# Attention units of four heads instead of two, a softmax in eight portions and a written order on all engines, in a fused attention and MoE kernel

## The chip, the cores and the metric

The kernel runs on one core of a Trainium2 chip. The metric is the device time of one execution in microseconds (us). The engines are named as in the profile: PE (TensorE: matrix products, PEld its weight loads), DVE (VectorE), ACT (ScalarE), POOL (GpSimd) and SP (SyncE, which here only issues transfers).

## The reference, cut to what matters

Eight batches of eight heads, 512 local and 32 global tokens, head width 64; a local token sees the keys within 32 places of it and the 32 global ones, a global token sees all 544. The result, 4608 tokens by 512, goes through a gated feed-forward layer.

```python
k_all = np.concatenate([k_g, k_l], axis=2); v_all = np.concatenate([v_g, v_l], axis=2)
out_g = sm(scale * q_g @ k_all.T) @ v_all                    # global tokens
s_ll = np.where(np.abs(pos[:, None] - pos[None, :]) <= 32, scale * q_l @ k_l.T, -1e9)
out_l = sm(np.concatenate([scale * q_l @ k_g.T, s_ll], -1)) @ v_all   # local tokens
# x: both as rows of 512 (8 heads x 64)
xn = x / sqrt(mean(x * x) + 1e-6) * rms_g
g = xn @ w_gate
return (g * sigmoid(g) * (xn @ w_val)) @ w_out               # 512 -> 1536 -> 512
```

## The kernel before

**Chunks.** The tokens go through the feed-forward part (MoE) in nine chunks: chunks 0 to 7 are the local tokens of one batch each (512), chunk 8 the 256 global ones. The attention of chunks 0 and 1 runs at the head of the program, together with the conversion of the weights, in an order written by hand; that head ends about 171 us in, and the diff leaves its work alone. From then on PE works on the MoE of chunk c, and the attention of chunk c+1 is put between its products. The change concerns the attention of chunks 2 to 7, so six chunks, and the global units that lie between.

**MoE of a chunk.** 72 half-steps of six dense products (128 rows by 512 columns, fp16, each operand split into a high and a low part): for each of twelve feature tiles f two half-steps of the gate product (bank `p0`) and two of the value product (`p1`), then 24 half-steps of the output product. Behind a tile's gate product ACT takes the tanh (`moe_gate`), DVE makes the gate from it ("gate"); behind its value product DVE multiplies (`moe_h`, "inner"), ACT casts the high part, POOL subtracts for the low part. `p0` has one PSUM bank, so the next tile's gate product waits until "gate" has read it, and the same holds for `p1` and "inner".

**Slots.** After each half-step `slot()` may issue steps of the attention from the list `todo`. A step is ready when its unit's first slot has come (`UNIT`) and when the steps it names are a given number of slots back; at most one step that uses PE goes into a slot. So in a chunk the places before are: local units start at slots 0, 20, 30 and 40 and the global one at 10; for the first unit loads L at slot 0, scores S at 4, values A at 11; for the global unit scores GS at 14, transposes GT at 19, values GA at 23, the turn GX at 26.

**A local unit before** (`local_quarters`) has two heads and a quarter of the sequence on each 32 partitions. S: 64 products of 32 query rows by 128 keys into two PSUM banks. Softmax, issued with S: per 128 columns DVE adds the mask and takes the minimum of the negated scores, ACT takes the exponential and its sum, adds a small number to the sums, DVE inverts them, POOL multiplies 128x512 by them, DVE transposes in blocks of 32. A: per block of keys and quarter a product for each head into four banks, 56 products of one to four query tiles (32 columns each). A product in fp32 appears in the trace as two matmul records in A, as one in S. Then four DVE copies of 128x128 and the squares on ACT, summed by POOL. `attn_bank` hands out four PSUM banks; scores, values, GS and GA all take them, and each waits until a bank has been read empty.

**Order.** PE and SP run in the order in which the program is written. DVE, ACT and POOL are ordered by a scheduler from chunk 1 on, with the MoE's instructions ahead (`HIGH`).

Of the kernel before, what the change touches and what calls it, by code (L numbers as in the profile page):

```python
# [9 lines left out]
F32 = mybir.dt.float32  # L10
# [55 lines left out]
def attention_moe_kernel(  # L66
# [37 lines left out]
    with tc.high_priority(100000):  # L104
        mask = con.tile([P, 4 * P], F32, tag="mask", name="mask")
# [315 lines left out]
    def local_unit(c, hp):  # L421
# [12 lines left out]
        def load():  # L434
# [4 lines left out]
            else:  # L439
                q = pool.tile([P, SL], F32, tag="q", name=f"q{u}")  # L440
                k = pool.tile([P, KU], F32, tag="k", name=f"k{u}")
# [69 lines left out]
        def copies(h):  # L511
            st["pt", h] = pool.tile([P, 512], F32, tag="pt", bufs=2, name=f"pt{u}{h}")
            nc.scalar.copy(st["pt", h], st["t", h])

        def values():
            ps = st["a"] = bank(f"a{u}", "pg" if hp % 2 == 0 else "pv")
            for g in range(4):
                for h in range(2):
                    for a in range(4):
# [4 lines left out]
                            st["pt", h][:, i * QT : (i + 1) * QT],  # L524
# [39 lines left out]
    def local_quarters(c, b, hp, xt):  # L564
        u = b * (H // 2) + hp
        w = u - EARLY * (H // 2)
        st = {}

        def load():
            if w == 0:  # L570
                late["mask"] = con.tile([P, 4 * P], F32, tag="mask", name="maskb")
                nc.sync.dma_start(late["mask"], maskb)
                nc.sync.dma_start(same, eyes)
            q = pool.tile([P, SL], F32, tag="q", name=f"q{u}")
            nc.sync.dma_start(q, qkb[w, :, :SL])
            k = pool.tile([P, 1024], F32, tag="v", bufs=4, name=f"k{u}")[:, : 4 * KB]
            nc.sync.dma_start(k, qkb[w, :, SL:])
            v = pool.tile([P, 1024], F32, tag="v", bufs=4, name=f"v{u}")[:, : 4 * KB]
            nc.sync.dma_start(v, vb[w])
            st.update(q=q, k=k, v=v)  # L580

        def softmax(h, ps):
            sm = st["sm"]
            e = pool.tile([P, 4, P], F32, tag="e", bufs=4, name=f"e{u}{h}")
            for g in range(4):
                cols = slice(g * P, (g + 1) * P)
                nc.vector.tensor_tensor_reduce(  # L587
                    out=e[:, g, :],
                    in0=ps[:, cols],
                    in1=late["mask"][:, cols],  # L590
# [4 lines left out]
                    accum_out=sm[:, 0, 4 * h + g : 4 * h + g + 1],  # L595
                )
            for g in range(4):
                j = 4 * h + g
# [4 lines left out]
                    bias=sm[:, 0, j : j + 1],  # L603
                    scale=-1.0,
                    accum_out=sm[:, 1, j : j + 1],
                )
            r = sm[:, 2, 4 * h : 4 * h + 4]
# [652 lines left out]
```

## Time and profile before

| | |
|---|---|
| time, median of 3 executions | 976.73 us (976.18 to 977.36) |
| the profiled execution | 977.08 us, its span 975.1 us |
| mean granted TensorE clock | 0.989 of full speed |
| PE | 940.9 us busy, 96% of the span |
| DVE, ACT, POOL | 457.9, 403.1 and 198.2 us busy |

The profile shows one execution; the 2 us between its time and its span lie before the first and after the last instruction. An engine's busy time is the union of its instructions. PE's matmuls are pipelined: a record is longer than the distance to the next one, so the distance of two starts is what a product costs.

### The profile page before, as it was taken

To read this page: it belongs to the slowest core of one execution; us is meant where nothing else is said; L and a number is where in the kernel's file an instruction comes from. 1 tells how busy PE (TensorE), PEld (TensorE's weight loads), DVE (VectorE), ACT (ScalarE), POOL (GpSimd) and SP (SyncE) were. 2 spreads that over 40 slices of the span, in tenths; PEclk is the share of its full clock that TensorE was granted. 3 is DMA by queue.
4 is the path that set the end of the run, shared out by engine and by line. 5 is a ranking of instruction groups with operands and counts; after the bars stand their busy time and mean duration, and the time that the engine had idled before them with its cause. 6 is when DMAs were issued, how large, how long until landed. Compare 5 with 4: busy or idle time off the path is not lost.

```text
span 975.1 us, 24168 instructions
## 1 busy us (share of the span) xinstructions
PE 940.9 (96%) x10308; PEld 489.4 (50%) x10308; DVE 457.9 (47%) x1417; ACT 403.1 (41%) x1070; POOL 198.2 (20%) x183
## 2 busy tenths in 40 slices
PE   6588999999999999999999999999999999999998
PEld 4444455455445554455445454455445544444584
DVE  6999973434344443434343534434433534332231
ACT  7999982344133431444133531445134421332131
POOL 0000000223112331223131331233121421112020
PEclk9699999999999999999999999999999999999999
DMA  9972420800053101700052101610071102400100
GB/s 358 405 260 87 157 89 33 267 31 21 23 155 109 51 2 41 245 31 21 23 179 87 50 13 62 214 50 2 24 224 56 35 12 99 126 1 1 44 1 22
DMA packets 31258, 90.55 MB, mean 93 GB/s; under 512 B 3632, under 2 KB 3888, under 8 KB 31152
## 3 DMA queue, kind: packets, MB, share of 16 engines
q1 hardware_dynamic: 30720, 88.68, 27.0%
q8 instruction: 81, 1.33, 0.6%
q10 hardware_dynamic: 432, 0.33, 0.1%
q14 instruction: 25, 0.20, 0.1%
HBM read 80.09 MB, written 8.91 MB: 91 GB/s over the span
## 4 chain that ended last, share of the span: by engine, by line
PE 86%; DVE 6%; DMA 5%; ACT 2%; issue 0%; SPq 0%; ACTq 0%; DVEq 0%
PE p L896 48%; PE po L945 24%; PE a L658 4%; PE po L1010 3%; PE s L626 3%; DMA k<-in_qk_dram 2%; DMA v<-in_vw_dram 1%; DMA wr<-in_w_in_dram 1%; PE ga L763 1%; PE gt L749 1%; PE gs L710 1%; DVE wf L366 1%; ACT wr L265 1%; DMA gkq<-in_gkq_dram 1%; DVE t L979 1%; DMA k<-in_qkb_dram 1%
## 5 line engine op out<-in xcount | busy, mean ns | idle before, releaser
L896 PE MATMUL p<-xh,wf 128*128 128x512 f16 (+1 forms) x1728 | 505.5, 368 | 6.9 <-DVE t L979 6.3
L896 PEld LDWEIGHTS <-wf 128*128 128x128 f16 x2592 | 248.8, 98 | 275.9 <-issue 19.9
L896 PE MATMUL p<-xl,wf 128*128 128x512 f16 (+1 forms) x864 | 317.9, 368 | 0.2 <-DVE xl L821 0.2
L945 PE MATMUL po<-wo,h 128*128 128x512 f16 x1080 | 236.4, 379 | 0.0
L151 POOL TENSOR_TENSOR h<-t,h 128x512 f16<-128x512 f32 (+1 forms) x96 | 105.2, 1095 | 463.4 <-ACT h L917 460.8
L945 PEld LDWEIGHTS <-h 128*128 128x128 f16 x1080 | 105.1, 98 | 124.5
L907 DVE SCALAR_TENSOR_TENSOR t<-t,p 128x512 f32<-128x512 f32 (+1 forms) x96 | 62.4, 650 | 162.8 <-ACT t L906 162.8
L917 ACT CAST h<-t 128x512 f16<-128x512 f32 (+1 forms) x96 | 56.6, 589 | 147.2 <-DVE t L914 147.2
L906 ACT ACTIVATE t<-p,half_inv 128x512 f32<-128x512 f32 (+1 forms) x96 | 62.9, 655 | 124.7 <-PE p L896 109.7
L914 DVE SCALAR_TENSOR_TENSOR t<-t,c_h,p 128x512 f32<-128x512 f32 (+1 forms) x96 | 68.5, 714 | 72.4 <-PE p L896 72.3
L599 ACT ACTIVATE e<-e,sm 128x128 f32<-128x128 f32 x192 | 74.3, 389 | 44.1 <-DVE sm L587 44.1
L610 POOL TENSOR_TENSOR e<-e,sm 128x512 f32<-128x512 f32 x48 | 49.1, 1039 | 130.9 <-DVE sm L609 106.0
L587 DVE CUSTOM_DVE_ANT_0 e<-s,maskb 128x128 f32<-128x128 f32 x192 | 42.5, 286 | 38.5 <-PE s L626 38.5
L957 DVE TENSOR_SCALAR o<-po,kk 128x512 f32<-128x512 f32 x15 | 11.3, 751 | 103.6 <-PE po L945 103.6
L886 ACT CAST xh<-x 128x512 f16<-128x512 f32 x24 | 14.0, 615 | 82.7 <-DVE x L883 82.7
L613 DVE STREAM_TRANSPOSE et<-e 128x512 f32<-128x512 f32 x48 | 34.1, 710 | 25.1 <-POOL e L610 25.1
L658 PEld LDWEIGHTS a<-et,v 32*64 32x64 f32 x2688 | 35.5, 130 | 10.2 <-issue 10.2
L151 POOL TENSOR_TENSOR xl<-x,xh 128x512 f16<-128x512 f32 x12 | 18.6, 1549 | 98.3 <-ACT xh L886 98.3
L669 ACT ACTIVATE sq<-x 128x512 f32<-128x512 f32 x24 | 15.1, 630 | 56.6 <-DVE x L667 56.6
L658 PE MATMUL a<-et,v 32*64 32x64 f32 (+3 forms) x2688 | 38.2, 242 | 0.0
L599 ACT ACTIVATION_READ_ACCUMULATOR e<-e,sm 128x1 f32 x192 | 36.1, 188 | 0.0
L667 DVE COPY x<-a 128x128 f32<-128x128 f32 x96 | 21.2, 283 | 24.6 <-PE a L658 24.6
(320 smaller groups left out, 752.8 us busy)
## 6 DMA issues: line engine op xcount, KB each, us to landing
wr<-in_w_in_dram SPq DMA_DIRECT2D x24, 512.0 KB, 9.7
k<-in_qkb_dram SPq DMA_DIRECT2D x24, 448.0 KB, 6.8
v<-in_vb_dram SPq DMA_DIRECT2D x24, 448.0 KB, 5.0
gkq<-in_gkq_dram SPq DMA_DIRECT2D x16, 576.0 KB, 6.6
out_dram<-o SPq DMA_DIRECT2D x34, 256.0 KB, 2.0
v<-in_vw_dram SPq DMA_DIRECT2D x16, 512.0 KB, 9.9
gv<-in_gv_dram SPq DMA_DIRECT2D x16, 448.0 KB, 10.2
wr<-in_w_out_dram SPq DMA_DIRECT2D x12, 512.0 KB, 4.5
```

What stands on the lines that cost most here:

```text
L151: nc.gpsimd.tensor_tensor(dst, a, b, ALU.subtract)
L587: nc.vector.tensor_tensor_reduce(out=e[:, g, :], in0=ps[:, cols], in1=late["mask"][:, cols], scale=-0.125, scalar=3.0e38, op0=ALU.add, op1 ...
L599: nc.scalar.activation(e[:, g, :], e[:, g, :], AF.Exp, bias=sm[:, 0, j : j + 1], scale=-1.0, accum_out=sm[:, 1, j : j + 1],)
L610: nc.gpsimd.tensor_tensor(e, e, r.unsqueeze(2).to_broadcast([P, 4, P]), ALU.mult)
L613: nc.vector.transpose(st["et", h], e.rearrange("p g k -> p (g k)"))
L658: nc.tensor.matmul(o, st["v"][a * QT : (a + 1) * QT, m * P + h * D : m * P + (h + 1) * D], x, start=(m == blocks[0]), stop=(m == blocks[-1 ...
L896: nc.tensor.matmul(ps[:, :n], wf[f][:, a, o : o + P], ch[z][k][:, :n], start=(k == 0 and i == 0), stop=(k == NK - 1 and i == 2),)
L906: nc.scalar.activation(t[:, :n], pg[:, :n], AF.Tanh, scale=half_inv[:, f : f + 1])
L907: nc.vector.scalar_tensor_tensor(t[:, :n], t[:, :n], 1.0, pg[:, :n], ALU.add, ALU.mult)
L914: nc.vector.scalar_tensor_tensor(t[:, :n], t[:, :n], c_h[:, f : f + 1], pv[:, :n], ALU.mult, ALU.mult)
L917: nc.scalar.copy(h[:, 0, :n], t[:, :n])
L945: nc.tensor.matmul(ps[0], ch["h", f][:, a, j * P : (j + 1) * P], wo[f][:, z, :], start=(f == 0 and q == 0), stop=(f == NF - 1 and q == 2),)
```

## The change

From chunk 2 on a local unit (`local_halves`) has four heads, as two pairs (z), with half a sequence on each 32 partitions; a chunk has two such units instead of four. The keys of a score product come from both pairs' tiles, so S (128 products, four banks) needs the queries and keys of both; the values are a load of their own (V). A pass over values has 11 blocks of keys (88 products for four heads; 112 before): the first block, the global keys, serves eight query tiles (256 columns), the others three, two or one. They run in two pieces, A (5 blocks) and B (6). The copies are of 128x256, two for each pair: X for the first, Y for the second. The softmax is cut into eight portions, M0, N0 to M3, N3 (two times 128 columns each), with the division D and the transposes T of a bank as steps of their own. The same steps of a chunk now stand at: loads 0 and 2, S 6, M0 7, N0 8, M1 9, D0 and N1 10, M2 11, T0, D1 and N2 12, M3 13, T1, D2 and N3 14, T2 and D3 16, T3 18, A 19, B 21, X 22, GS 23, Y 24, then the globals' softmax GM 24 and GN 26, GT 29, GA 33, GX 36, and the second unit's S 37, A 50, B 52, X 53, Y 55.

All five engines run in the written order. In it the half-step's products come first, then the slot's steps, then the gate, inner or store that belongs to the half-step (`rest`). The norm's last part issues its four scalings, four casts and four subtractions together, in three groups. The mask has six instead of four blocks of 128 columns (393 KB instead of 262, loaded once).

```diff
-    HIGH = 10
+    SPLIT, BGAP = 5, 2
-    UNIT = {0: 0, 2: 20, 3: 16, 4: 12, 5: 10, 6: 9, 7: 8}
+    UNIT = {2: (0, 20), 3: (2, 19, 33)}
...
-    def local_quarters(c, b, hp, xt):
+    def local_halves(c, b, hp, xt):
...
+            for z in range(2):
+                q = pool.tile([P, SL], F32, tag="q", name=f"q{u}{z}")
+                nc.sync.dma_start(q, qkb[2 * w + z, :, :SL])
+                k = pool.tile([P, 1024], F32, tag="v", bufs=4, name=f"k{u}{z}")[:, : 4 * KB]
+                nc.sync.dma_start(k, qkb[2 * w + z, :, SL:])
...
+        def divide(x, bk):
...
             nc.vector.reciprocal(r, r)
             nc.gpsimd.tensor_tensor(e, e, r.unsqueeze(2).to_broadcast([P, 4, P]), ALU.mult)
...
+            ps = [[attn_bank(f"s{u}{x}{bk}") for bk in range(2)] for x in range(2)]
...
+            for t in range(8):
+                bk, g = divmod(t, 4)
+                for z in range(2):
+                    for half in range(2):
...
+                            nc.tensor.matmul(
+                                ps[x][bk][p : p + QT, g * P : (g + 1) * P],
+                                st["q"][z][r, i * QT : (i + 1) * QT],
+                                st["k"][z][r, k0 : k0 + P],
...
+        blocks = (10, 2, 3, 4, 5, 6, 7, 1, 8, 0, 9)
+
+        def values(ms):
...
+            for m in ms:
+                for p in range(4):
+                    r = slice(p * QT, (p + 1) * QT)
+                    for x in range(2):
+                        lo, n, e = queries(st["et"][x][r], m)
...
-            for a in range(4):
-                nc.vector.tensor_copy(xt[hp][:, a * P : (a + 1) * P], ps[a][:, :P])
...
+        def take(z):
...
+            for half in range(2):
+                nc.vector.tensor_copy(
+                    x[:, half * 256 : (half + 1) * 256], st["a"][2 * z + half][:, :256]
+                )
...
+            ("L", load, 0, [("^S", 0)]),
+            ("V", load_v, 0, [("^B", 0)]),
+            ("S", scores, 1, [("L", LG[0]), ("^Y", 1)]),
+        ]
+        for j, (x, bk) in enumerate(((0, 0), (1, 0), (0, 1), (1, 1))):
+            steps += [
+                (f"M{j}", lambda x=x, bk=bk: softmax(x, bk, (0, 1)), 0, [("S", 2 * j + 1)]),
+                (f"N{j}", lambda x=x, bk=bk: softmax(x, bk, (2, 3)), 0, [(f"M{j}", 1)]),
+                (f"D{j}", lambda x=x, bk=bk: divide(x, bk), 0, [(f"N{j}", 2)]),
+                (f"T{j}", lambda x=x, bk=bk: turn(x, bk), 0, [(f"D{j}", 2)]),
+            ]
+        return steps + [
+            ("A", lambda: values(blocks[:SPLIT]), 1, [("T3", 1), ("V", 4)]),
+            ("B", lambda: values(blocks[SPLIT:]), 1, [("A", BGAP)]),
+            ("X", lambda: take(0), 0, [("B", 1)]),
+            ("Y", lambda: take(1), 0, [("X", 2)]),
         ]
...
-            ("GT", transp, 1, [("GS", GG[1])]),
+            ("GM", lambda: softmax(0), 0, [("GS", 1)]),
+            ("GN", lambda: softmax(1), 0, [("GM", 2)]),
+            ("GT", transp, 1, [("GN", GG[1] - 2)]),
             ("GA", values, 1, [("GT", GG[2])]),
-            ("GX", turn, 1, [("GA", GG[3])]),
+            ("GD", divide, 0, [("GA", 1)]),
+            ("GX", turn, 1, [("GD", GG[3] - 1)]),
...
-            if i == 1:
-                if w == 0:
-                    ps["t"] = moe_gate(f, n, ps[0])
-                else:
-                    moe_h(ch, f, n, ps["t"], ps[1], on)
...
+        return [
+            (lambda: half(0, 0), None),
+            (lambda: half(0, 1), gate),
+            (lambda: half(1, 0), None),
+            (lambda: half(1, 1), inner),
+        ]
...
-    ctx.enter_context(tc.manual_schedule(engines={eng.PE, eng.SP}))
-    with tc.manual_schedule(engines={eng.DVE, eng.Activation}):
-        for name in ORDER.split():
-            job.pop(name)()
+    every = {eng.PE, eng.SP, eng.DVE, eng.Activation, eng.Pool}
+    ctx.enter_context(tc.manual_schedule(engines=every))
+    for name in ORDER.split():
+        job.pop(name)()
...
-        for k, w in enumerate(work):
-            with tc.high_priority(HIGH):
-                w()
+        for k, (products, rest) in enumerate(work):
+            products()
...
+            if rest:
+                rest()
```

DVE around the first copies of chunk 2, before; `a80` to `a83` are the four banks of A's result, `t2` and `t3` feature tiles 2 and 3, `gs000` and the like a global unit's four score banks:

```order
L907 SCALAR_TENSOR_TENSOR t2_2337<-t2_2337,p0_2_2324 128x512
L914 SCALAR_TENSOR_TENSOR t2_2337<-t2_2337,c_h_78,p1_2_2340 128x512
L667 COPY x2_0_2367<-a80_2368 128x128
L667 COPY x2_0_2367<-a81_2369 128x128
L667 COPY x2_0_2367<-a82_2370 128x128
L667 COPY x2_0_2367<-a83_2371 128x128
L907 SCALAR_TENSOR_TENSOR t3_2447<-t3_2447,p0_3_2434 128x512
L719 ISA ge0_2458,gsm0_2457<-gs000_2459,zeros_73 128x272
```

The same engine after, from the gate of tile 5 on, with the copies of X (`x2_0`) and Y (`x2_1`):

```order
L970 SCALAR_TENSOR_TENSOR t5_2592<-t5_2592,p0_5_2531 128x512
L704 COPY x2_0_2602<-a40_2473 128x256
L704 COPY x2_0_2602<-a41_2474 128x256
L977 SCALAR_TENSOR_TENSOR t5_2592<-t5_2592,c_h_78,p1_5_2595 128x512
L704 COPY x2_1_2645<-a42_2475 128x256
L704 COPY x2_1_2645<-a43_2476 128x256
L774 ISA ge0_2614,gsm0_2613<-gs000_2615,zeros_73 128x272
L774 ISA gsm0_2613 128x1
L774 ISA ge0_2614,gsm0_2613<-gs001_2616,zeros_73,gsm0_2613 128x272
```

Before, the four copies freed all of A's banks in one go, ahead of the gate of tile 3 and of the first reader of GS. Now X's two copies and Y's two have the inner of tile 5 between them, and GM, the first reader of GS, stands directly behind Y. On PE the eight GS products into `gs000` and `gs010` (which take the banks that X frees) and then the eight into `gs001` and `gs011` (those that Y frees) stand directly behind the last half-step of tile 5, the one that inner reads.

ACT in chunk 2, the first unit's softmax before; L599 are exponentials, L608 the small addition, L906 tanh, L917 casts:

```order
L917 CAST h0_2225<-t0_2209 128x512
L599 ACTIVATE e80_2271,sm8_2236<-e80_2271,sm8_2236 128x128 x4
L599 ACTIVATE e81_2285,sm8_2236<-e81_2285,sm8_2236 128x128
L906 ACTIVATE t1_2305<-p0_1_2229,half_inv_77 128x512
L599 ACTIVATE e81_2285,sm8_2236<-e81_2285,sm8_2236 128x128 x3
L608 ACTIVATE sm8_2236<-sm8_2236 128x4 x2
L917 CAST h0_2225<-t1_2305 128x512
```

ACT after, in the middle of the same softmax (L610, L619, L969 and L980 are the same four operations; `e410`, `e401` and `e411` three of the four banks, `t2` and `t3` tiles 2 and 3):

```order
L610 ACTIVATE e410_2350,sm4_2247<-e410_2350,sm4_2247 128x128 x2
L969 ACTIVATE t2_2355<-p0_2_2332,half_inv_77 128x512
L610 ACTIVATE e410_2350,sm4_2247<-e410_2350,sm4_2247 128x128 x2
L619 ACTIVATE sm4_2247<-sm4_2247 128x4
L610 ACTIVATE e401_2378,sm4_2247<-e401_2378,sm4_2247 128x128 x2
L980 CAST h2_2383<-t2_2355 128x512
L610 ACTIVATE e401_2378,sm4_2247<-e401_2378,sm4_2247 128x128 x2
L619 ACTIVATE sm4_2247<-sm4_2247 128x4
L610 ACTIVATE e411_2408,sm4_2247<-e411_2408,sm4_2247 128x128 x2
L969 ACTIVATE t3_2413<-p0_3_2387,half_inv_77 128x512
L610 ACTIVATE e411_2408,sm4_2247<-e411_2408,sm4_2247 128x128 x2
L619 ACTIVATE sm4_2247<-sm4_2247 128x4
```

Before, eight exponentials stood around one tanh, and the rest of the chain was the MoE's own; now sixteen stand in pairs between the tanh and the casts of tiles 1 to 3, and each engine keeps to this order whichever operand is ready first.

## Rows read from the trace of the kernel before

**Rows 1.** Table by stage: 250 to 550 us, three stretches of 100, summed.

```profile
sum 300.00, PE 299.69 PEld 149.46 DVE 126.17 ACT 101.54 POOL 76.73; mean PE 99.90 PEld 49.82 DVE 42.06 ACT 33.85 POOL 25.58
```

**Rows 2.** Chain of waits, one chunk: start us, us, what, records.

```profile
387.88 6.47 PE p L896 x30
394.36 1.09 PE s L626 x64
...
404.62 1.52 PE a L658 x77
406.14 3.99 PE p L896 x18
...
417.79 1.09 PE gt L749 x10
...
483.33 12.96 PE po L945 x60
```

**Rows 3.** Timeline, PE: end of a values run: start us, us, what.

```profile
345.23 0.75 PE L658 MATMUL a<-et,v 32*64 32x96 f32 x44
```

**Rows 4.** Page, groups of instructions: busy us, mean ns | idle before.

```profile
L658 PE MATMUL a<-et,v 32*64 32x64 f32 (+3 forms) x2688 | 38.2, 242 | 0.0
...
L667 DVE COPY x<-a 128x128 f32<-128x128 f32 x96 | 21.2, 283 | 24.6 <-PE a L658 24.6
```

**Rows 5.** Timeline, PE: around a GS and the half-step behind it.

```profile
409.75 0.38 PE L896 MATMUL p<-xh,wf 128*128 128x512 f16 x1
...
411.14 0.39 PE L896 MATMUL p<-xh,wf 128*128 128x512 f16 x1
...
412.23 0.59 PE L896 MATMUL p<-xh,wf 128*128 128x512 f16 x2
```

**Rows 6.** Timeline, DVE: copies, and the inner behind that half-step.

```profile
406.03 0.88 DVE L667 COPY x<-a 128x128 f32<-128x128 f32 x4 [0.63 <-PE a L658]
...
412.64 0.75 DVE L914 SCALAR_TENSOR_TENSOR t<-t,c_h,p 128x512 f32<-128x512 f32 x1 [0.15 <-PE p L896]
```

**Rows 7.** Timeline, DVE: a softmax and the MoE operations in it.

```profile
395.48 0.29 DVE L587 CUSTOM_DVE_ANT_0 e<-s,maskb 128x128 f32<-128x128 f32 x1 [1.64 <-PE s L626]
...
398.45 0.69 DVE L907 SCALAR_TENSOR_TENSOR t<-t,p 128x512 f32<-128x512 f32 x1 [1.19 <-ACT t L906]
399.48 0.75 DVE L914 SCALAR_TENSOR_TENSOR t<-t,c_h,p 128x512 f32<-128x512 f32 x1 [0.34 <-PE p L896]
400.14 0.24 DVE L609 RECIPROCAL sm<-sm 128x4 f32<-128x4 f32 x2
...
402.46 0.71 DVE L613 STREAM_TRANSPOSE et<-e 128x512 f32<-128x512 f32 x1 [0.29 <-POOL e L610]
```

**Rows 8.** Timeline, ACT: the same softmax.

```profile
397.76 0.66 ACT L906 ACTIVATE t<-p,half_inv 128x512 f32<-128x512 f32 x1
398.33 0.39 ACT L599 ACTIVATE e<-e,sm 128x128 f32<-128x128 f32 x1
...
399.48 0.33 ACT L608 ACTIVATE sm<-sm 128x4 f32<-128x4 f32 x2
400.26 0.62 ACT L917 CAST h<-t 128x512 f16<-128x512 f32 x1 [0.44 <-DVE t L914]
```

**Rows 9.** Timeline, POOL: the same softmax.

```profile
400.39 2.04 POOL L610 TENSOR_TENSOR e<-e,sm 128x512 f32<-128x512 f32 x2 [4.66 <-DVE sm L609]
402.38 1.16 POOL L151 TENSOR_TENSOR h<-t,h 128x512 f16<-128x512 f32 x1
```

**Rows 10.** Tile gkq, 389 to 392 us: issues, and time to landing.

```profile
L689 SPq DMA_DIRECT2D gkq<-in_gkq_dram x2: 422/422/422, 390.5 to 391.0; - x2
...
DMA to landing us min/median/max: 6.1/7.1/8.1
```

**Rows 11.** Tile gkq, 497.4 to 500 us: the same.

```profile
L689 SPq DMA_DIRECT2D gkq<-in_gkq_dram x2: 430/430/430, 499.3 to 499.8; - x2
...
DMA to landing us min/median/max: 7.9/8.8/9.8
```

More of the change, by code (lines that the diff above doesn't have):

```diff
@@ L511, in copies @@
         def copies(h):
[L512 to L513 removed]
+            if "pt" not in st:
+                st["pt"] = pool.tile([P, 1280], F32, tag="gpt", bufs=1, name=f"pt{u}")
+            nc.scalar.copy(st["pt"][:, h * 512 : (h + 1) * 512], st["t", h])
         def values():
@@ L928, in half, with gate, inner @@
             moe_in(ch, w, f, n, ps[w], range(2 * i, 2 * i + 2))
-            if i == 1:
-                if w == 0:
-                    ps["t"] = moe_gate(f, n, ps[0])
-                else:
-                    moe_h(ch, f, n, ps["t"], ps[1], on)
-        return [lambda w=w, i=i: half(w, i) for w in range(2) for i in range(2)]
+        def gate():
+            ps["t"] = moe_gate(f, n, ps[0])
+        def inner():
+            moe_h(ch, f, n, ps["t"], ps[1], on)
+        return [
[3 more added lines that the diff above has]
+            (lambda: half(1, 1), inner),
+        ]
     def moe_block(ch, j, row):
@@ L951, in part, with store @@
                     )
-            if i == NF // 2 - 1:
-                o = pool.tile([P, DM], F32, tag="t", bufs=3, name=f"o{j}")
-                if j % 2 == 0:
-                    nc.scalar.mul(o, ps[0], inv_k)
-                else:
-                    nc.vector.tensor_scalar(o, ps[0], inv_k, None, ALU.mult)
-                nc.sync.dma_start(out[row + j * P : row + (j + 1) * P, :], o)
-        return [lambda i=i: part(i) for i in range(NF // 2)]
+        def store():
+            o = pool.tile([P, DM], F32, tag="t", bufs=3, name=f"o{j}")
+            if j % 2 == 0:
+                nc.scalar.mul(o, ps[0], inv_k)
+            else:
+                nc.vector.tensor_scalar(o, ps[0], inv_k, None, ALU.mult)
+            nc.sync.dma_start(out[row + j * P : row + (j + 1) * P, :], o)
+        last = NF // 2 - 1
+        return [(lambda i=i: part(i), store if i == last else None) for i in range(last + 1)]
     def first_chunk():
@@ L1039, in attention_moe_kernel @@
     for c in range(NCH):
-        units = [(c, hp, "local") for hp in range(H // 2)] if EARLY <= c < B else []
+        units = [(c, hp, "local") for hp in range(H // 4)] if EARLY <= c < B else []
         for i, g in enumerate(gplan[c]):
-            units.insert((i + 1) * len(units) // 3 + i, (g,))
+            units.insert(i + 1, (g,))
         for i, un in enumerate(units):
             if len(un) == 3:
-                xi, steps = un[1], local_quarters(c, c, un[1], chunks[c]["x"])
+                xi, steps = 2 * un[1], local_halves(c, c, un[1], chunks[c]["x"])
             else:
```

240 lines of the change are left out of this document (127 added, 113 removed).

## The prediction

> **What bounds the kernel now.** First the table by stage: from 250 to 550 us PE is busy for 299.69 of 300 us, and no other engine for half of that [rows 1]. Behind the head nothing is gained by making another engine shorter; the time can fall only through less PE work in the six changed chunks, and rise through more of it or through new waits of PE. Then the chain of waits, which in a chunk is PE alone. One chunk there runs from 387.88 to 483.33 + 12.96 = 496.29 us, 108.41 us [rows 2]. The reader should see two prices in it. 60 dense products take 12.96 us, 0.216 each, a half-step of six 1.296. And a run of attention products costs its own row and a little more: the 18 dense products behind a values run take 3.99 us instead of 3.89 [rows 2], so 0.10 is added to each run. A score step S is then 1.09 + 0.10 = 1.19, a values step A 1.52 + 0.10 = 1.62.
>
> **What the change takes away.** Scores: a product of 128 fp32 columns costs 0.109, as the ten transposes GT in 1.09 us show [rows 2]. The 64 products of S use eight parts of the array side by side (two row halves, four column quarters), so they are eight rounds, 8 x 0.109 = 0.87, and the remaining 0.32 is the price of going into and out of a run. Four heads at once are 16 rounds, 0.32 + 1.74 = 2.06. A chunk had four at 1.19 (4.76) and gets two at 2.06 (4.12): it saves 0.64 us.
>
> Values: 56 products, two matmul records each, on eight parts are 14 rounds in 1.62 - 0.30 = 1.32 us, with S's fixed share as the nearest price of a run. Two of the rounds have 128 columns (0.22 together), so the twelve of 32 to 96 columns take 0.092 each, whatever their width. That they are this flat is read from the end of a run: its last 44 records, 5.5 rounds, span 0.75 us [rows 3], of which the last record's own 0.24 [rows 4] comes off: 0.51, and 5.5 x 0.092 is 0.51. Paid by columns (0.109 / 128 each; 96, 64 and 32 wide) they would be 0.29; by columns and a fixed 0.032 a round, which also gives 1.32 for the run, 0.46. A unit of four heads now has 22 rounds: two of 256 columns (0.22 each) and 20 short ones, in two runs: 0.60 + 0.44 + 1.84 = 2.88 instead of 2 x 1.62 = 3.24. It saves 0.36 a unit, 0.72 a chunk. The bounds: with the fixed 0.032 a round only 0.19 a unit; at a price for each product (1.32 / 56) 0.56; by columns alone nothing, since their number is the same. I take 0.36, by the row of 44.
>
> Together 1.36 a chunk, **8.2 us** in six.
>
> The Trainium skill, TensorEngine Tiling (Array Packing), section Instruction Overhead, says that a matmul of one column takes as long as one of 60. Were that floor, about 0.025 us at 2.4 GHz, all that short products pay, rounds of 32 columns would hardly feel it and fewer rounds would save nothing; the 0.51 measured against 0.29 speaks against it.
>
> **The wait that it adds.** In the new order GS stands directly behind the last half-step of feature tile 5, and the second half of its products needs the two banks that Y's copies empty. On DVE these stand behind the inner of that tile, which reads the half-step that PE has only just issued. So from the end of the half-step on PE: DVE starts inner at 412.64 where PE issued the last product at 412.23 + 0.22, so 0.19 later [rows 5, 6]. Inner holds DVE for 0.66 (399.48 to 400.14, [rows 7]). A copy of 128x256 isn't in the trace; the four of 128x128 follow each other by (0.88 - 0.28) / 3 = 0.20 and take 0.28 [rows 4, 6], the 128x512 inner, which reads PSUM too, 0.66 and 0.75 [rows 6, 7]. By columns between them: 0.35 to the second copy and 0.44 for it. Sum 0.19 + 0.66 + 0.35 + 0.44 = 1.64 us. Until then PE has only the first half of GS: all of GS costs 411.14 - 409.75 - 0.22 = 1.17 [rows 5], half 0.58. PE waits 1.05 us in each of six chunks, **6.3 us**. Bounds: copies at the price of 128 columns give 0.75 a chunk (4.5), at that of 512 1.67 (10.0). Queued behind the waiting GS is the whole MoE; on DVE the next in line, GM, waits for GS, and is not late for GT, five slots on. In before the four copies were through at 406.03 + 0.88 [rows 6], 2.8 us ahead of the last dense product in front of GS, and nothing of this was there.
>
> **The softmax in written order.** Counted from the end of the half-step in slot 7, with exponentials 0.38 apart ((399.48 - 398.33) / 3), 0.77 for a pair, 0.23 for the small sum and its wait for the last exponential, tanh 0.66, cast 0.51 to 0.62 [rows 8], gate 0.69, minimum 0.29 [rows 7] and 0.03 for a handover (inner ends at 399.48 + 0.75, the cast starts at 400.26 [rows 7, 8]). ACT has the inner of tile 1 at 0.95, casts until 1.49, N0 and sum until 2.49, M1 3.26, tanh of tile 2 3.95; DVE its gate, the inversion and N1's minima until 5.00; ACT N1 and sum until 6.00, M2 6.77, cast 7.28, N2 and sum 8.28, M3 9.05, tanh of tile 3 9.74; the gate of tile 3 ends at 10.45. PE wants that bank eight half-steps on, at 10.37, and waits 0.1. Then, from 10.37 on, DVE turns a bank (T1, 0.64), inverts and takes the minima for N3 until 11.4, ACT N3 and sum until 12.4 and the cast of tile 3 until 13.1, POOL that tile's low part (1.16) and the last division (1.02, [rows 9]) until 15.3, DVE T3 (0.71, [rows 7]) until 16.0. A is wanted at 12 x 1.296 + 0.1 = 15.65. It is 0.3 late if its run waits before all else, nothing if the 0.30 that going into a run costs lies ahead of the first product that needs T3's tile, the second one. I take 0.1. So 0.2 a chunk, **1.2 us** (0.6 to 2.4). In before nothing of the MoE stood behind the softmax, since the scheduler put it first.
>
> **The loads.** S needs four transfers, 1,408 KB by the tiles' shapes, at seven half-steps, 9.07 us after a chunk's start. In before the fourth issue is the first gkq, with 1,728 KB up to its end: landed at 390.5 + 6.1 = 396.6 [rows 10], 8.7 after the start at 387.88. In one chunk of the six that I looked at it was 499.3 + 7.9 = 507.2 [rows 11], 10.9 after 496.29. The new fourth load is smaller by a fifth; in that one chunk it is late by nothing to 1.8. I take **0.8 us** in all.
>
> Edits at no cost: the second unit's portions meet the tanh and casts of other half-steps, with the four exponentials of a bank in one piece and so fewer changes of engine; were it as late as the first, another 1.2 us. GM and GN fill gaps of DVE and ACT, which are idle for more than half [rows 1]. The regrouped norm has six half-steps of cover, and a subtraction's length to pay if that were gone; the larger mask is loaded once, in the head.
>
> **Sum.** -8.2 + 6.3 + 1.2 + 0.8 = +0.1 us, against the profiled 977.08 us: 977.2. That execution lies 0.35 above the median, so 976.8. Runs of this kernel tell a difference from none at about 0.2%, 1.95 us.
>
> **Rivals.**
> - *Gains larger, chain on time.* If values are paid by the product, -0.20 a unit or 2.4 us, and the softmax's 1.2 falls away since a handover in rows is short, 973.2 us; copies at the price of 128 columns take another 1.8 off. For it: the 0.2 of the softmax is a difference of two sums of some 10 us. Against it: the flat 0.092 fits the 44 records.
> - *No wait at GS.* If I misread the order and Y's banks are not GS's, 970.5. The order of the copies speaks against it.
> - *The other side: the written order makes the softmax longer.* ACT and DVE hand over to each other or to POOL some ten times between slot 7 and A, and none may take what is ready instead. At 0.05 more for each PE waits another 0.5 a chunk, 979.8 us; at 0.1, 982.8. It decides from 0.33 a chunk. For it: the chain has no slack in my sum, so each delay counts in full. Against it: the one handover in rows is 0.03.
> - *Values paid by columns.* With the fixed 0.032 a round the gain shrinks by 0.17 a unit, 978.8; by columns alone it is gone, 981.1. The latter is what the Trainium skill's floor (TensorEngine Tiling (Array Packing), Instruction Overhead) would make of it. Against both: [rows 3].
>
> **Chances.** The forecast, with its own range of 974.8 to 978.8, 0.40; larger gains 0.27; no wait 0.06; a longer softmax 0.16; values by columns 0.11, half of it beyond the bound. So faster by over 0.2% 0.35 (0.27 + 0.06, and a little of the forecast's edge), within 0.43, slower 0.22. The range from 971 to 981 leaves out the case without a wait, the larger gains with everything on their side, and the worse half of the longer softmax.
>
> **What would show it.** In the chain of waits of after: S of 128 records with about 1.96 us, two of them in a chunk; A and B together about 2.7 (2.88 less the added 0.1 of each). In the waits of PE a row of GS released by the copies, DVE x, six times, 1.05 each. Small waits of p released by the gate's t, and of a by the transposes et, 0.1 each. A chunk of 108.3 to 108.5 us. I am wrong if GS waits for nothing or for twice as long, if a waits for et by 0.5 or more, or if A and B together are below 2.5 or over 3.0 us.

## The result, and the profile after

The median is 982.50 us (978.90 to 984.27, six executions), before's beside it 976.47 (976.17 to 977.36). The ratio is 1.0056, interval 1.0044 to 1.0068: the change makes the kernel slower by half a per cent, where 976.8 was forecast and 981 was the upper end. Two things are in this number. The profiled execution took 978.90 us, only 1.8 more than before's 977.08. And the executions now spread over 5 us where before's stayed within 1.2, with the profiled one at their low end. (In the later comparisons, with 11 to 21 executions each, before's spread over 1.9 to 3.5 us, so only a spread well beyond 3 says something.)

The chain of waits of after, the chunk that answers to [rows 2]:

```profile
389.62 9.06 PE p L959 x42
398.69 1.99 PE s L648 x126
400.68 17.09 PE p L959 x78
417.77 1.69 PE a L691 x56
419.45 2.70 PE p L959 x12
422.15 1.24 PE a L691 x71
423.39 2.71 PE p L959 x12
...
426.13 0.75 DVE t L977
426.87 0.34 DVE x L704
...
427.36 1.02 PE gs L762 x16
428.37 7.88 PE p L959 x36
...
468.10 1.47 PE a L691 x66
...
472.27 1.24 PE a L691 x71
...
498.36 1.73 PE p L959 x8
```

It is 498.36 - 389.62 = 108.74 us long, before 108.41. S has 1.99 (+ 0.10 that the next dense stretch shows), 2.09 where 2.06 was expected. The second unit's A and B take 1.47 and 1.24, the first's A 1.69, so 0.22 more. From the end of the dense stretch at 423.39 + 2.71 to the next at 428.37 GS takes 2.27 us, where a GS by itself has 1.08; the chain leaves PE there for the inner (`t`) and a copy (`x`). And 78 products behind the first S take 17.09 instead of 78 x 0.216 + 0.10 = 16.95: 0.14 of waiting for tile 3's gate, which ends at 412.37, 0.06 before PE goes on there.

The waits of PE, over the whole run: engine, line waited for, us in total, times, longest.

```profile
PE p L959 <- DVE t L1050: 6.3, 6, 2.5
PE gs L762 <- DVE x L704: 3.9, 6, 0.7
...
PE p L959 <- issue: 1.4, 1, 1.4
```

The first row is before's too, with the same 6.3 us. The second is the wait that the order of DVE makes: 0.65 each, six times. The last row is new as well and stood in no step of the prediction: once, 1.4 us, with no releaser that the trace shows ("issue"). It stands behind the first S after the head, at 181.75, where the half-step that follows has all that it needs.

The timelines around the first GS, PE and DVE:

```profile
208.24 0.38 PE L959 MATMUL p<-xh,wf 128*128 128x512 f16 x1
208.55 0.69 PE L762 MATMUL gs<-gkq 64*32 64x272 f32 x16
209.89 1.02 PE L762 MATMUL gs<-gkq 64*32 64x272 f32 x16 [0.65 <-DVE x L704]
210.84 0.39 PE L959 MATMUL p<-xh,wf 128*128 128x512 f16 x1
```

```profile
206.11 0.75 DVE L704 COPY x<-a 128x256 f32<-128x256 f32 x2
208.66 0.75 DVE L977 SCALAR_TENSOR_TENSOR t<-t,c_h,p 128x512 f32<-128x512 f32 x1 [1.80 <-PE p L959]
209.32 0.75 DVE L704 COPY x<-a 128x256 f32<-128x256 f32 x2
```

The reader sees inner waiting for the half-step (208.66), the two copies of Y behind it (0.75 for both, so until 210.07), and the second half of GS: it starts at 209.89, behind the first of the two copies, and the next dense product follows at 210.84, so the half takes 0.95 instead of 0.58. From the last dense product at 208.24 to the next at 210.84 less 0.22 is 2.38; before it was 1.17 [rows 5]. The half-step's last product was issued by 208.24 + 0.22 = 208.46, and the copies were through 1.61 us after that, where 1.64 was summed; from there the rest of GS takes 0.77 instead of the 0.58 of the sum.

### The profile page after: what moved, and what is told of

Its sections match the earlier page's. It is cut to its first block, busy times and chain, and to the rows that moved or that the text cites. A ratio compares the mean times of both kernels' runs of the same rounds, so it can differ in the third digit from the quotient of the medians.

```text
span 977.1 us, 22949 instructions
## 1 busy us (share of the span) xinstructions
PE 939.2 (96%) x9732; PEld 486.3 (50%) x9732; DVE 451.0 (46%) x1369; ACT 409.2 (42%) x1070; POOL 194.4 (20%) x183
## 4 chain that ended last, share of the span: by engine, by line
PE 86%; DVE 6%; DMA 5%; ACT 2%; issue 1%; SPq 0%; ACTq 0%; DVEq 0%
PE p L959 48%; PE po L1014 24%; PE a L691 3%; PE po L1081 3%; PE s L648 2%; DMA k<-in_qk_dram 2%; DMA v<-in_vw_dram 1%; DMA wr<-in_w_in_dram 1%; PE ga L819 1%; PE gt L805 1%; PE gs L762 1%; DVE wf L366 1%; ACT wr L265 1%; DMA gkq<-in_gkq_dram 1%; DVE t L1050 1%
## 5 line engine op out<-in xcount | busy, mean ns | idle before, releaser
L1014 PE MATMUL po<-wo,h 128*128 128x512 f16 x1080 | 237.4, 379 | 0.0
L980 ACT CAST h<-t 128x512 f16<-128x512 f32 (+1 forms) x96 | 56.5, 588 | 164.8 <-DVE t L977 164.8
L969 ACT ACTIVATE t<-p,half_inv 128x512 f32<-128x512 f32 (+1 forms) x96 | 62.9, 656 | 115.8 <-PE p L959 100.5
L610 ACT ACTIVATE e<-e,sm 128x128 f32<-128x128 f32 x192 | 74.8, 390 | 40.6 <-DVE sm L599 40.6
L1025 ACT ACTIVATE o<-po,kk 128x512 f32<-128x512 f32 x15 | 10.3, 688 | 114.2 <-PE po L1014 114.2
L599 DVE CUSTOM_DVE_ANT_0 e<-s,maskb 128x128 f32<-128x128 f32 x192 | 45.0, 281 | 5.6 <-PE s L648 5.6
L691 PEld LDWEIGHTS a<-et,v 32*64 32x64 f32 x2112 | 31.0, 130 | 11.0 <-issue 10.2
L610 ACT ACTIVATION_READ_ACCUMULATOR e<-e,sm 128x1 f32 x192 | 35.8, 186 | 0.0
L691 PE MATMUL a<-et,v 32*64 32x96 f32 (+3 forms) x2112 | 35.5, 258 | 0.0
L704 DVE COPY x<-a 128x256 f32<-128x256 f32 x48 | 17.5, 416 | 38.2 <-PE a L691 38.2
L1081 PE MATMUL po<-wo,h 128*128 128x512 f16 x144 | 32.4, 379 | 0.0
```

Source lines behind the costliest of these rows:

```text
L599: nc.vector.tensor_tensor_reduce(out=e[:, g, :], in0=ps[:, g * P : (g + 1) * P], in1=late["mask"][:, m * P : (m + 1) * P], scale=-0.125, s ...
L610: nc.scalar.activation(e[:, g, :], e[:, g, :], AF.Exp, bias=sm[:, 0, j + g : j + g + 1], scale=-1.0, accum_out=sm[:, 1, j + g : j + g + 1],)
L691: nc.tensor.matmul(o, st["v"][x][r, m * D : (m + 1) * D], e, start=(m == blocks[0]), stop=(m == blocks[-1]), skip_group_check=True,)
L969: nc.scalar.activation(t[:, :n], pg[:, :n], AF.Tanh, scale=half_inv[:, f : f + 1])
L980: nc.scalar.copy(h[:, 0, :n], t[:, :n])
L1014: nc.tensor.matmul(ps[0], ch["h", f][:, a, j * P : (j + 1) * P], wo[f][:, z, :], start=(f == 0 and q == 0), stop=(f == NF - 1 and q == 2),)
```

## The experiments

All times are medians (lowest to highest) of executions, beside executions of before on the same chip; a ratio is to before, with its interval. Two questions stood at the start: what the waits in a chunk cost, and whether the spread of the executions comes from the waits at GS (theory 1) or from something else that is new (theory 2, its rival).

**The change again, and the order of two copies.** The same kernel (`after_again`), and Y one slot earlier, so that DVE has its copies ahead of the inner (`y_before_gs`):

```diff
-            ("Y", lambda: take(1), 0, [("X", 2)]),
+            ("Y", lambda: take(1), 0, [("X", 1)]),
```

> The changed kernel once more. Its profiled execution took 978.9 us with the granted clock at 1.00 in every stretch behind the head, and its six executions lay between 978.9 and 984.3 while those of before lay within 1.2 us. Theory 1: the profile's own 1.8 us over before are new waits (GS behind the copies of Y, 1.09 us a chunk), and the rest of the median, 3.6 us, is stretches at a lower granted clock, which start behind that wait of PE. Theory 2: such stretches come, but from something else that is new, the score runs of 2 us above all. By both: executions scattered again over some 5 us, median 981 to 983.5; a profile above 980 shows a granted clock under 1.00 behind the head, one at 979 does not.

> Y one slot earlier (its distance to X is 1 slot instead of 2), so that DVE has the copies of Y before the inner of tile 5 and nothing of GS waits for that inner. Both theories: a chunk falls from 108.73 to 107.64 us, the profiled execution to 972.4. Theory 1: with PE's wait the low-clock stretches are gone too, so median 972 to 973 and executions within 1.5 us. Theory 2: the scatter stays, median about 976, executions over some 5 us.

Measured: 981.30 us (979.20 to 985.61) for the change, ratio 1.0046 (1.0029 to 1.0064); 973.95 (971.24 to 975.03) for the earlier Y, 0.9964 (0.9952 to 0.9976). Its chain in the chunk that answers to the one above:

```profile
398.06 1.99 PE s L648 x123
...
422.76 2.70 PE p L959 x12
425.46 1.08 PE gs L762 x32
426.54 7.88 PE p L959 x36
...
505.58 1.99 PE s L648 x123
```

GS has its own 1.08 again, and from S to the next chunk's S it is 505.58 - 398.06 = 107.52 us. So the six waits at GS cost 1.2 us each, 7 in all, and without them the change is faster than before. The scatter went from 6.4 to 3.8 us, where theory 1 expected 1.5 and theory 2 some 5; that settles nothing, and the last runs below speak for another place.

**Values in one run** (`one_run`), A's slot left empty:

```diff
-            ("A", lambda: values(blocks[:SPLIT]), 1, [("T3", 1), ("V", 4)]),
-            ("B", lambda: values(blocks[SPLIT:]), 1, [("A", BGAP)]),
+            ("A", lambda: None, 1, [("T3", 1), ("V", 4)]),
+            ("B", lambda: values(blocks), 1, [("A", BGAP)]),
```

> Values of a unit in one run at B's slot; A's slot is left empty. By my price of 0.30 for going into and out of a run 12 runs less save 3.6 us, and the unit-0 wait for T3 (0.22 a chunk, 1.3 us) goes since the run starts two half-steps later: profile 974.0 if undisturbed. If going into a run costs nothing that can be saved: 977.6. Theory 1: GS still waits 1.09 a chunk, so the executions stay scattered and the median is 3 to 4 us above an undisturbed profile. Theory 2: the same, unless the pairs A and B were the source, then no scatter.

Measured: 978.63 (977.57 to 983.02), 1.0025 (1.0014 to 1.0037); the profile 977.58. From S at 401.32 to S at 509.22 it is 107.90 us instead of 108.74: 0.84, of which 0.60 are the two runs at 0.30 and 0.22 the wait for T3. The price of a run holds: in the second unit alone, where A waits for nothing, the two runs give 1.47 + 1.24 + 0.20 = 2.91 and the one run 2.51 + 0.10, 0.30 less. That the profile meets the 977.6 of a run without a price is chance: it shows 5.4 us of PE waiting without a releaser, 3.0 behind the first S and two more of 2.4 together inside values runs of 176 records, which the change has not; most of the gain of the chunks (some 5 us) is given back there. The first of the two, with its table by stage:

```profile
204.41 2.41 PE L691 MATMUL a<-et,v 32*64 32x256 f32 x165
208.08 0.33 PE L691 MATMUL a<-et,v 32*64 32x32 f32 x11 [1.26 <-issue]
```

```profile
204.00:206.00 2.00, 2.00 (x111) 1.51 (x111) 0.69 (x1) 0.69 (x1) 0.56 (x1) 1.00 0.04 8
206.00:208.00 2.00, 0.82 (x78) 0.71 (x64) 0.43 (x1) 0.00 (x0) 0.00 (x0) 1.00 0.00 0
```

The last three columns are the granted clock, the DMA engines' busy share and what they moved in GB/s: hardly any DMA runs here.

**The scheduler's order** (`scheduled`): the change, with DVE, ACT and POOL ordered by the scheduler as before.

```diff
-    every = {eng.PE, eng.SP, eng.DVE, eng.Activation, eng.Pool}
-    ctx.enter_context(tc.manual_schedule(engines=every))
+    ctx.enter_context(tc.manual_schedule(engines={eng.PE, eng.SP}))
...
+            with tc.high_priority(10):
+                products()
```

> The four-head units and eight portions as they are, but DVE, ACT and POOL ordered by the scheduler again, with the MoE ahead (priority 10), as before the change. Its order has the copies of Y before the inner of tile 5. Theory 1: the waits at GS (1.09), for tile 3's gate (0.14) and for T3 (0.22) are gone, 1.45 a chunk, 8.7 us: profile and median 970 to 971, executions within 1.5 us. Theory 2: profile 970 to 971, median 3 to 4 above, scattered. A third case, in which the written order is what keeps the softmax in time: a or GT waits for the softmax by more than 0.5 us a chunk, 974 or more.

Measured: 989.96 (989.48 to 990.01), 1.0131 (1.0118 to 1.0144), the third case. Its waits of PE:

```profile
PE p L959 <- DVE t L970: 8.1, 9, 1.3
...
PE p L959 <- DVE t L977: 4.9, 2, 2.7
```

ACT runs all sixteen exponentials of a unit in one go, from 560.75 on for 6.5 us with only the small sums between, and the chain of waits has the MoE's `t` behind them: PE waits 2.2 us for it here, and 2.7 at another place. So in these units it is the written order that keeps the MoE in time; left to this scheduler, it isn't. The table by stage of that place (PEclk is the granted clock as a share of 2.4 GHz):

```profile
566.00:568.00 2.00, 0.27 (x2) 0.00 (x0) 1.33 (x5) 1.55 (x10) 1.05 (x2) 1.00 0.00 0
568.00:570.00 2.00, 1.51 (x6) 0.69 (x6) 1.71 (x3) 1.21 (x2) 2.00 (x3) 0.83 0.00 0
570.00:572.00 2.00, 2.00 (x7) 0.67 (x5) 0.72 (x2) 0.00 (x0) 0.52 (x1) 0.50 0.00 0
572.00:574.00 2.00, 2.00 (x9) 0.83 (x8) 0.75 (x1) 0.25 (x1) 0.00 (x0) 0.82 0.00 0
574.00:576.00 2.00, 2.00 (x11) 0.88 (x9) 0.00 (x0) 0.75 (x2) 1.16 (x1) 1.00 0.00 0
```

PE stands still until 568.5 and then runs at 0.50, 1.2 GHz, for some 3 us. This wait cost more than its length.

**A longer wait at GS** (`long_wait`): the change with Y's copies written three times.

```diff
-            for half in range(2):
+            for again in range(3 if z == 1 and hp == 0 else 1):
+                for half in range(2):
```

> The changed kernel with the two copies of Y in the first unit of each chunk written three times, the same values again, so DVE has four copies more between the inner of tile 5 and the end of Y. Theory 1 (a wait of PE costs its length, and in some executions a stretch at the lower clock behind it): the wait in GS grows from 0.65 to about 2.05 us, 1.4 a chunk, 8.4 us in all: an undisturbed profile at 987.3; the lower clock then comes in more chunks or in all six, at some 2 us each, so median 991 to 999, and the trace shows a granted clock under 1.00 right behind GS. Theory 2 (the low-clock stretches have nothing to do with this wait): median 990 to 991.5, the 982 of the change plus 8.4.

Measured: 993.15 (992.35 to 995.51), 1.0172 (1.0158 to 1.0186). The wait is 2.0 each in the list, a chunk 110.05 us in two of the four between the first and the last, and 111.7 in the other two: there the clock falls to 0.50 right behind GS, as it does behind the first S. So behind a wait of 2 us the lower clock came in two chunks of six, 1.7 us each time; that it comes behind one of 0.65 was not shown by this.

**A and T3** (`t3_later`), on top of the earlier Y:

```diff
-    SPLIT, BGAP = 5, 2
+    SPLIT, BGAP = 5, 1
-            ("A", lambda: values(blocks[:SPLIT]), 1, [("T3", 1), ("V", 4)]),
+            ("A", lambda: values(blocks[:SPLIT]), 1, [("T3", 2), ("V", 4)]),
```

> On top of the earlier Y: A one slot later behind T3, and B directly behind A, so B, X, Y and GS stay where they are. Theory 1: the 0.22 that A of the first unit waits for T3 goes, 1.3 us: a chunk 107.3 instead of 107.52, median 972.6 against 973.95; the copies' way is unchanged. Rival: A's extra time is not a wait but the price of a run with its first products at work on another unit's tiles, then nothing changes, 107.5 and 974.

Measured: a chunk 107.30 us (397.70 to 505.00 between two S) against 107.52, so the 0.22 is a wait and is gone. The median is 974.86 (971.81 to 978.25), 0.9983 (0.9971 to 0.9995): the 1.3 us don't show in it, they are under the scatter. A second trace of it (`t3_look`) was meant to place that:

> The version with A later and B directly behind it once more, for a trace. Its executions lay between 971.8 and 978.3 though PE waits for nothing at GS. If little work on the array is enough to lower the clock, a stretch at 0.5 stands behind A, B and GS, which there follow each other with only three half-steps between; if a wait is needed, behind the first S alone.

It took 971.22 us with the clock at 1.00 throughout and tells nothing of it.

**Scores in two steps** (`s_split`), on top of the earlier Y: `scores(0)` and `scores(1)`, four of the eight query tiles each, in neighbouring slots.

```diff
-            for t in range(8):
+            for t in range(4 * part, 4 * part + 4):
...
-            ("S", scores, 1, [("L", LG[0]), ("^Y", 1)]),
+            ("S", lambda: scores(0), 1, [("L", LG[0]), ("^Y", 1)]),
+            ("S2", lambda: scores(1), 1, [("S", 1)]),
```

> On top of the earlier Y: the 128 score products of a unit in two steps of 64, in neighbouring slots. By my price of a run (0.32) 12 runs more cost 3.8 us: 977.8 by that alone. The wait of PE without a shown cause behind the first S of the program (1.4 to 3.0 us, in each version with four heads, in none of before): if PE runs out of instructions behind 256 short ones in a row, it goes, so 975 to 976.5; if it has to do with the loads of that moment, it stays. For the scatter of the earlier-Y version (971.2 to 975.0): if long runs of small products start a stretch at the lower clock, executions lie within 2 us here.

Measured: 974.38 (973.46 to 976.30), 0.9977 (0.9967 to 0.9988). The wait without a releaser is 0.6 instead of the 2.8 of the earlier Y, and a chunk takes 505.06 - 397.20 = 107.86 us, 0.34 more. Two units at 2 x (1.09 + 0.10) instead of 2.09 are 0.58 more, so the price of a run, 0.29, is there again; the first unit's waits for the gate and for T3 are 0.24 shorter in return.

**Further traces of the change**, to place a lower clock (`after_third`, `after_fourth`, `after_fifth`):

> The changed kernel for a third trace. Theory 1: if this execution is above 980, a granted clock below 1.00 stands behind one or more of the waits of PE (GS, or the one behind the first S), and nowhere else behind the head; if it is at 979, the clock is at 1.00 throughout.

> The changed kernel for a fourth trace, to see where a stretch at the lower clock stands. Where the execution is above 981: granted clock of 0.5 for 3 to 4 us, behind GS (its 0.65 of waiting between two pieces of small products) or behind the first S, each about 1.7 us of time. At 979 to 981: clock 1.00 throughout and only the wait behind the first S longer.

> The same as the fourth look at the changed kernel, in case that one is undisturbed: stretches of the lower clock behind GS or the first S above 981 us, none below.

980.95, 979.60 and 979.34 us, in each the clock at 1.00 behind the head, and 2.9, 2.5 and 2.5 us of waiting behind the first S. The first has a stop 1.5 us longer than the first profile's, and took 2.05 us more; none placed a lower clock.

**What the runs point to** (`combined`): the earlier Y, values in one run, and the first S of the program in two steps.

> Earlier Y, values of a unit in one run at B's slot, and the scores of the very first four-head unit in two steps. From the profiles: a chunk of the one-run version takes 107.90 us with the wait at GS, the earlier Y took 108.73 - 107.52 = 1.21 off, so 106.7; six chunks are 10.3 us under before's 108.41, and the wait behind the first S shrinks to 0.6: 966.5 to 968 undisturbed. Theory as it stands now (the lower clock comes behind a wait of PE, or where little but small products runs for some us): values in one run of 2.6 us and GS two half-steps later have no wait, median 967 to 969. Rival: the long values run lets PE run out of instructions or brings the lower clock: median 970 to 973, scattered.

Measured: 970.08 us (967.74 to 973.23) against 977.15, 0.9936 (0.9923 to 0.9950). It beats before by 7 us, and lies some 11 below the medians of the change on other chips. Behind its first S there is no stop in the trace, but two waits without a releaser, 2.4 together, stand inside values runs of 176 records, so the median falls into the rival's 970 to 973.

**The two waits apart.** `after_first_split` is the change with its first S alone in two steps, `y_first_split` has the earlier Y as well:

```diff
+            ("S", lambda: [scores(p) for p in range(2 if w else 1)], 1, [("L", LG[0]), ("^Y", 1)]),
+            ("S2", lambda: None if w else scores(1), 0 if w else 1, [("S", 0 if w else 1)]),
```

> The changed kernel with the scores of its first four-head unit alone in two steps, so that the wait of PE behind the first S (1.4 to 2.9 us in five traces of the change) is gone and the six waits at GS stay. If the lower clock of the change's executions starts behind the waits at GS: an undisturbed profile at 977.0 to 977.5 and a median still 2 to 4 us above it, 979.5 to 981, with clocks down to 0.984. If it starts behind the wait at the first S: median within 1 us of the profile, 977 to 978.5, clocks 0.988 to 0.990.

> Both: the earlier Y and the first scores in two steps, values in two runs as in the change. Neither wait is left, so by both theories executions within 2 us of each other, at 971.5 to 972.5 (973.95 of the earlier Y less some 2 us). If it scatters over more than 3 us with clocks under 0.987, something that no wait of these two explains lowers the clock.

979.19 (978.29 to 982.97), 1.0023 (1.0014 to 1.0032), and 971.97 (971.14 to 975.09), 0.9951 (0.9937 to 0.9964). Each has one execution far above its others, the next are 980.29 and 972.43: neither expectation for the first is met in full, and the 2 us for the second are missed by that one. Since the chip was another one than for the change, the four combinations ran once more on one chip (`both_waits` is the change, `first_s_wait_only` the earlier Y):

> A two by two on one chip: the changed kernel, with both waits. If the wait behind the first S starts the lower clock: median 981 to 983, two executions in three with a clock of 0.988 or less. If it depends on the chip and not on the kernel's waits: median within 1 us of 979.3, its undisturbed profiles.

> The first scores in two steps, GS waiting as in the change. First-S theory: median 979 to 979.5, clocks 0.989 to 0.990 but for one execution or two. GS theory: median 2 to 4 us above 979, as the changed kernel beside it.

> The earlier Y, the first S in one step. First-S theory: the lower clock stays in many executions, median 2 to 3 us above the version with neither wait. GS theory: no lower clock; only the wait behind the first S itself, 1 to 2.5 us more than with neither.

> Neither wait: median 971.5 to 972.5, executions within 2 us but for one or two, by both theories.

| median us (lowest to highest) | first S in one step | first S in two steps |
|---|---|---|
| GS waits | 981.70 (979.33 to 982.58) | 978.53 (977.80 to 980.37) |
| earlier Y | 974.75 (971.78 to 978.25) | 972.48 (971.60 to 973.01) |

Before on that chip: 977.13. The waits at GS cost 6.1 to 7.0 us, the first S in one step 2.3 to 3.2. The spread is 3.3 and 6.5 us in the left column, 2.6 and 1.4 in the right, but two of the four cells have only five executions. Over all versions with 11 or 12 it is 5.5 to 6.5 us with the first S in one step (three) and 2.6 and 4.7 with it in two, the 4.7 with that one execution; so the first S makes most of the spread, and not all of it. In both profiles of the left column the lower clock stands right behind the first S, in both of the right nowhere behind the head; of all 13 traces with the first S in one step three have it there, of the six with it in two none. That place in the change, timeline of PE and table by stage:

```profile
180.57 2.12 PE L648 MATMUL s<-k,q 64*32 64x128 f32 x128
185.68 0.61 PE L959 MATMUL p<-xh,wf 128*128 128x512 f16 x1 [2.99 <-issue]
186.08 0.63 PE L959 MATMUL p<-xl,wf 128*128 128x512 f16 x1
```

```profile
180.00:182.00 2.00, 2.00 (x103) 1.53 (x106) 0.86 (x2) 0.12 (x1) 0.00 (x0) 1.00 1.01 412
182.00:184.00 2.00, 0.69 (x45) 0.42 (x31) 0.34 (x4) 0.88 (x4) 0.00 (x0) 1.00 1.10 342
184.00:186.00 2.00, 0.32 (x1) 0.13 (x2) 0.00 (x0) 0.00 (x0) 0.00 (x0) 0.78 1.05 223
186.00:188.00 2.00, 2.00 (x6) 0.76 (x5) 0.00 (x0) 0.00 (x0) 0.00 (x0) 0.50 0.99 235
188.00:190.00 2.00, 2.00 (x9) 0.83 (x8) 1.54 (x9) 0.76 (x2) 0.07 (x1) 0.87 1.06 260
190.00:192.00 2.00, 2.00 (x11) 0.87 (x9) 0.05 (x2) 1.97 (x10) 1.09 (x1) 1.00 1.03 345
```

PE stops for 2.99 us behind 128 score products, then the clock is at 0.78 and 0.50 until about 188.5. From this S to the second unit's S it is 54.88 us here and 51.95 in the first profile, 2.93 more: 1.60 of it the longer stop, 1.33 the clock. DMA is busy at a share of 1.0 all the while.

**What the traces say of the stop.** The page's section on DMA has a queue of the kind "instruction", q8. It moved 76 packets of 16 KB in the change and 81 in before; the traces have 19,598 and 20,745 instructions of PE (products, weight loads, and some 130 others, semaphores above all), so by these counts it brings PE's instructions, some 256 in a packet. Before's trace has a stop of this kind too, in the head, behind 52 records of a values run:

```profile
28.70 0.42 PE L522 MATMUL a<-v,pt 128*32 128x64 f32 x12 [0.85 <-issue]
```

And this is the DMA of the microsecond from 205 to 206 in the version with values in one run, ahead of the stop that ends at 208.08:

```profile
q8 instruction: 1, 0.02, 8.6%
```

The one packet is busy for 8.6% of 16 engines' microsecond, 1.38 us, from 205.47 to 206.85; PE goes on 1.23 us behind its end.

The packets and instructions of the traces show the same at every stop of PE without a releaser of 0.2 us or more, 47 in the 20 traces: PE goes on 1.2 to 1.6 us behind the end of a packet of q8, and counted from the program's start the first instruction behind a stop is always the 706th, 962nd, 3,778th, 4,290th or 7,874th, which lie whole multiples of 256 apart. At the first S the packet moves from 180.64 to 181.63 in the first profile, where PE goes on at 183.14, and from 183.00 to 184.20 in the one above, where it goes on at 185.68. At the other places of this kind the packet had ended at least 1.26 us before PE came there. S hands PE 256 instructions in 2.06 us; the dense products need 128 x 0.216 = 27.6 us for as many. So PE stops because its next packet of instructions comes late.

## Why the prediction was wrong

The forecast, gains and new waits that cancel, names what changes in a chunk and comes near its length: it said 108.3 to 108.5 us, and it is 108.74, so that a chunk loses 0.33 where next to nothing was expected. It misses what happens outside the chunks.

- **Scores**: 0.64 a chunk expected, 4.76 - 4.18 = 0.58 measured. Right, to a tenth.
- **Values**: 0.36 a unit expected; A and B without the wait are 2.91 instead of 3.24, so 0.33. The run of 2.88 by the flat price of a round came out at 2.91; by the product it would have been 2.68, with the fixed 0.032 a round 3.05, by columns 3.24, so these rivals fall.
- **The wait at GS**: the mechanism was right, and the place; the size was 1.05 and is 1.19 to 1.21, 7.2 us instead of 6.3. The copies came in time; what was too small is the second half of GS, which after the second copy still takes 0.77 instead of 0.58. That it's held twice, once for each copy, fits this and was not taken apart.
- **The softmax in written order**: 0.2 a chunk expected, 0.14 for the gate and 0.22 for T3 measured, 2.2 us instead of 1.2. The reason for taking 0.1 at A, that the price of going into a run may lie under the wait, is not borne out. The rival of a longer softmax is not either: it needed 0.5 a chunk on top, 0.16 was measured. That the median lies by its 982.8 is chance.
- **The loads**: 0.8 us expected; the profile has no wait of S for `k`. In three other traces one of 0.2 to 0.5 stands there, once each.
- **Range and rivals**: the six chunks add 6 x 0.33 = 2.0 us to the profiled execution and the stop behind the first S 1.4; 1.0 of GS waiting for `gkq` and 0.3 of S for `k`, which before's list of waits has, are absent from this one. That is 2.1, and the spans differ by 977.1 - 975.1 = 2.0. The step that failed is "Behind the head nothing is gained ...; the time can ... rise through more of it or through new waits of PE": I looked for new waits only where an operand or a bank comes late, and priced each at its length. **The stop of PE behind the first S** was in no term. It is 1.4 to 3.0 us, once in each version with S of 128 products in one step, and 0 to 1.8 with the first S in two; in a part of the executions the lower clock behind it comes on top. Cutting that S takes 2.3 to 3.2 us off the median. With that term the forecast would have been 979 to 980; with the terms above at their measured sizes too (scores 0.4, values 0.4, GS 0.9, softmax 1.0 more, loads 0.8 less) 981.0 to 981.9, beside medians of 981.30 to 982.50. The sign of the stop was there to see: before's trace has one of 0.85 us in the head.

Between the first profile and that of the two by two lie 3.7 us: 1.60 of it the longer stop, 1.33 the clock, and 0.88 that the head took longer. So stop and clock can move an execution by some 3 us. The highest ones, 984.27 and 985.61, lie 5.4 and 6.7 above the first profile and have no trace: what they lost beyond that is open. So is why the version with A later spreads to 978 us; the earlier Y by itself spread as far in the two by two (971.78 to 978.25), so the later A is not needed for it.

Open is also why the packet comes late where it does. At the first S the DMA engines are full, but inside the values runs, where PE stops as well, their share is 0.04 and less: full DMA is not needed. No run moved a packet or the DMA on purpose.

The Trainium skill, TensorE: Matmul & The Clock Gate, section A second HAM failure mode: psum-queue depth-cycling, tells of a kernel in which PE idles briefly and often between groups of products, so that the clock goes back and forth and the time is lost in that. In these traces single stops of 2.0 to 3.0 us had the lower clock behind them in some cases; the six waits of 0.65 at GS had none behind them in any trace.

## What to carry to other kernels

In an order that is written for all engines, look for the instruction that frees a buffer and what stands ahead of it on its engine: here one slot's distance put two copies behind an operation that needs PE's newest result, and turned a gain of some 3 us into a loss of some 4.5. Merging small products into one long run saves the price of going in and out, but it also hands PE its instructions faster: look in and behind such runs for a stop of PE that nothing releases, and beside it at the packets of the instruction queue. Where executions spread, one profile is not the median: compare its time with the others before explaining the difference by it.

## What the runs showed of the hardware

- Twenty rounds of eight fp32 records side by side with 32 to 96 columns took (2.91 - 0.60 - 0.44) / 20 = 0.094 us each on average, with 0.60 for going into and out of two runs and 0.44 for two rounds of 256 columns; a round of 128 columns took 0.109.
- Going into and out of a run of such records between dense products cost 0.30 us (values in one run) and 0.29 (scores in two steps).
- Behind a stop of PE of 2.0 to 3.0 us the granted clock was at 0.50 for about 3 us in some executions and not in others, 1.3 to 1.7 us each; behind stops of 0.65 us it stayed at 1.00 in every trace.
- In or behind long runs of short products PE stopped for up to 3.0 us with no wait for a semaphore, each time until 1.2 to 1.6 us behind the end of a packet of its instructions.
